# Contiguous Fourier products, one tile left out and a newly searched instruction order in a one-core gated attention and Fourier kernel

## The chip, the cores and the metric

The kernel runs on one core of one Trainium2 chip. The metric is the device time of one launch in microseconds (us). "Before" is the tuned kernel that we start from, "after" is the changed one. Executions of this kernel come in a usual, fast state and in a slower one (over 1.5% above the fastest of the same kernel); the comparisons below use fast runs.

The engines are named as in the profile: PE is TensorE, PEld its weight loads, DVE is VectorE, ACT is ScalarE, POOL is GpSimd, SP is SyncE, which issues most of the transfers.

## The reference

The output mixes two branches of the same input x (2048 rows of 640) with one gate per row. Shapes and masks are cut here to what matters.

```
g = sigmoid((x * gate_w).sum(-1))             # one gate per row
# a: 32 heads of 20 columns, 4 segments of 512 rows, with a running memory
q, k, v = x @ wq, x @ wk, x @ wv
phi = lambda t: where(t > 0, t + 1, exp(t))
for s in range(4):
    p     = softmax(qs @ ks.T * scale + causal_mask)
    a_mem = (phi(qs) @ M) / (phi(qs) @ z)      # M and z are zero in segment 0
    o     = sig(beta) * a_mem + (1 - sig(beta)) * (p @ vs)
    M, z  = M + phi(ks).T @ vs,  z + phi(ks).sum()
a = o @ wo
# b: a spectral filter
b = irfft2(rfft2(x) * (w_r + 1j * w_i))
out = g * a + (1 - g) * b
```

The Fourier transforms are done as matmuls with tables of cosines and sines. Along the 640 columns there are products called D (forward) and Db (inverse); the even and odd symmetry of the input lets each half of a D result be summed from fewer rows.

## The kernel before

The kernel's text is not the order in which its instructions run. The text lists operations (a group of matmuls, an eviction, a transfer) with what they read and write. A list scheduler inside the kernel, called the planner below, then plays the program through when the kernel is built: it has a duration for every operation, starts what is ready by priority, chooses an engine where an operation allows two, gives out PSUM banks, and records what it started. The recorded order is the program. It is fixed: on the chip each engine runs its own list strictly in that order, and waits on semaphores.

```
class Sched:
    HOP = 70.0                        # ns from the end of an operation to its reader
    ...
    def schedule(self, pools, plan=(), nsem=56):
        for o in ops if plan else ():
            shift, pick = divmod(plan[o.key], 3)
            o.prio += shift / 10.0                         # a shift of the priority, us
            if pick and len(o.alts) > 1:                   # and perhaps a pinned engine
                o.alts = dict([list(o.alts.items())[pick - 1]])
        ...
        def try_dispatch(e):
            for idx, o in enumerate(ready[e]):             # sorted by (prio, id)
                if len(o.alts) > 1 and finish(o, e) > min(finish(o, q) for q in o.alts) + 1e-6:
                    continue                               # the other engine ends sooner
                ...
                fn, occ, lat = o.alts[e]
                if e == "pe":
                    occ *= self.pe_slow(now, occ)          # its model of the half clock
                busy_until[e] = now + occ
                ...
                self.order.append(o)
        ...
        self.makespan = max(o.t1 for o in ops)
```

PLAN is a literal of 1324 integers, one for each group of operations, the result of a long search outside the kernel. `makespan` is how long the program takes in the planner's own arithmetic. I shall call it the planned length.

The costs that the planner uses are written beside each operation, for example these two:

```
    def copy_alts(self, dst, src, n, ...):                 # PSUM evictions: either engine
        alts["act"] = (..., 100 + 0.833 * n, 95.0)         # ns occupied, ns of latency
        alts["dve"] = (..., 75 + 1.04 * n, 85.0)
    ...
    # phi: exp on ACT, then max(x, 0) + 1 and a min with the exponential on DVE
    self.Sc.op({"dve": (fmax, 75 + 0.26 * L, 85.0)}, ..., name="phi_max", lock=True)
```

The attention scores run as groups of 4 to 8 small matmuls on row-tiled quarters of the array; the gate tables, the first projections of q and k and the last output projection use column tiles; everything else uses the full array. The 80 score groups share PSUM banks 0 to 3 (one group holds all four), nearly everything else shares banks 4 to 7.

The D products, with their eviction (typ 0 is the cosine part, typ 1 the sine part; KD is 321):

```
    parts = ((0, 0, 2, 161, 0), (1, 0, 1, KD, 161), (2, 1, 2, 160, 482)) if typ == 0 else (
        (2, 1, 2, 160, 642), (3, 0, 1, KD, 802), (4, 0, 2, 161, 1123))
    for n_, (c, c0, st, n, tc) in enumerate(parts):        # chunk, first column, step, columns, table
        th = (self.ps(bank, c0, [st, n]), self.Ac.ap(...), big.ap(tc, [1, n]), n_ == 0, n_ == 2, ...)
        self.mms([(th, n)], ..., name="D")
    copy_alts(Bt.ap(typ * 322, [1, KD]), self.ps(bank, 0, [1, KD]))
```

The first and the third matmul of a group write every second PSUM column (step 2). And the first of the five q tiles of segment 0 is projected, evicted and stored, but nobody reads it.

Of the kernel before, what the change touches and what calls it, by code (L numbers as in the profile page):

```python
# [46 lines left out]
class Op:  # L47
    __slots__ = ("id", "alts", "preds", "succs", "prio", "banks", "nbytes", "npred", "eng", "t0", "t1",
                 "stamp", "need_inc", "dyn", "first", "outside", "name", "dma", "key", "xfer", "lock")


class Sched:
    HOP = 70.0
    WINDOW = 1600000
# [7 lines left out]
    def op(self, alts, r=(), w=(), prio=0.0, nbytes=0, name="", after=(), dma=False, xfer=0.0, lock=False):  # L62
# [6 lines left out]
        o.xfer, o.lock = xfer, lock  # L69
# [39 lines left out]
    def schedule(self, pools, plan=(), nsem=56):  # L109
# [50 lines left out]
        bw_free = port = 0.0  # L160
        sems = [[0.0, i, None] for i in range(nsem)]
# [37 lines left out]
        def try_dispatch(e):  # L199
            nonlocal bw_free, port  # L200
# [6 lines left out]
            for idx, o in enumerate(ready[e]):  # L207
# [31 lines left out]
                if e == "pe":  # L239
                    occ *= self.pe_slow(now, occ)  # L240
# [5 lines left out]
                if o.dma:  # L246
                    bw_free = max(bw_free + o.xfer, now + min(occ, 500.0) + o.xfer, now + occ)
                    tot, i = 0, len(issued) - 1
                    while i >= 0 and tot <= self.WINDOW:
                        tot += issued[i].nbytes  # L250
                        i -= 1
                    if i >= 0:
                        o.dyn.append(issued[i])
                    issued.append(o)
                    flight.append(o)
                    o.t1 = bw_free + 2000.0 + lat
                    sems.sort(key=lambda q: (q[0], q[1]))
                    sm = sems[0]
                    if sm[2] is not None:
                        o.dyn.append(sm[2])  # L260
                    sm[0], sm[2] = o.t1, o
                    o.stamp = sm[1]
                else:
                    o.t1 = busy_until[e] + lat
# [136 lines left out]
def make_tables():  # L401
# [27 lines left out]
    dtab = np.concatenate([C[0:128, 0::2], C[128:256], C[256:384, 1::2], Sn[256:384, 1::2], Sn[384:512], Sn[512:640, 0::2]], 1)  # L429
# [111 lines left out]
PECOL = 0.43  # L541
# [4 lines left out]
class Kern:  # L546
# [35 lines left out]
    def mms(self, items, r, w, prio, name="", extra=0.0):  # L582

        cost = sum(max(c * PECOL, 27.0) for _, c in items) + extra

# [6 lines left out]
        return self.Sc.op({"pe": (f, cost, 110.0)}, r=r, w=w, prio=prio, name=name)  # L592

    def copy_alts(self, dst, src, n, engines=("act", "dve"), scale=None):

        alts = {}
        if "act" in engines:
            alts["act"] = (lambda e: e.activation(dst(), src(), ACT.Copy), 100 + 0.833 * n, 95.0)  # L598
        if "dve" in engines:
            alts["dve"] = (lambda e: e.tensor_copy(dst(), src()), 75 + 1.04 * n, 85.0)  # L600
        return alts

    def one(self, eng, fn, n, r, w, prio, per=None, fix=None, name="", after=()):
        fix0, per0 = {"act": (100, 0.833), "dve": (75, 1.04), "pool": (100, 0.945)}[eng]
        per = per0 if per is None else per
        fix = fix0 if fix is None else fix
        return self.Sc.op({eng: (fn, fix + per * n, 90.0)}, r=r, w=w, prio=prio, name=name, after=after)

    def either(self, fn, n, r, w, prio, name="", after=()):

        return self.Sc.op({"dve": (fn, 75 + 0.52 * n, 90.0), "pool": (fn, 100 + 1.95 * n, 90.0)}, r=r, w=w, prio=prio, name=name, after=after, lock=True)

    def dma(self, dst, src, nbytes, r, w, prio, tr=False, name="", after=(), queue="sp", late=0.0):
        def f(e):
# [3 lines left out]
            with self.nc.allow_non_contiguous_dma(reason="small strided loads"):  # L618
                return e.dma_start(d_, s_)  # L619
        cost = 700.0 + nbytes / 260.0 if tr else 580.0 if nbytes in (41088, 163840) else 430.0  # L620
# [3 lines left out]
                          dma=True, xfer=xfer)  # L624
# [18 lines left out]
        -1614, -1515, -1314, -2268, -2070, -1866, -1878, -1863, -1857, -1815, -1893, -1920, -1356, -750, -231, 99, -3537, -3756, -4283, -4662, -3993,  # L643
        -5778, -5471, -6145, -1554, -2150, -1677, -1437, 189, -2325, -1686, -1374, -2244, -1446, -2277, 39, -3126, -2823, -1632, -3303, -2745, -2856,
        -2076, -1920, -501, -2677, -2334, -2523, -1608, -3204, -1269, -1425, -2984, -1443, -2109, -2759, -3747, -1299, -771, -598, -1323, -2676,
        -2895, -2262, -2847, -1956, -3894, -2832, -3426, -2853, -1347, -432, -757, -864, -3894, -2496, -2355, 1644, 333, 320, -1197, -3672, -2433,
        -3588, -1713, -453, -1851, -3522, -1638, -3057, -1476, -2532, -2439, -1170, -2562, -1761, -2136, -2295, -2844, -1737, -1143, -2541, -387,
        -1668, 1809, -1848, -4359, -2253, -1407, -4161, -3780, -2067, -3582, -3348, -2592, -3678, -2613, -2064, -3219, -3375, -1419, -1947, -1860,
        -3108, -969, -2403, -2538, -2370, -1395, -2427, -2349, -1611, -4107, -3411, -1839, -2328, -2346, -2016, -2661, -2484, -1812, -2409, -2679,
        -1545, -1095, -2184, -2613, -1272, -1026, -3231, -3852, -717, -1917, -2634, -1416, -2151, -1932, -945, -1695, -1923, -816, -555, -2313, -831,  # L650
        -747, -1362, -1002, -1896, -1917, -2424, 105, 498, -2214, -2139, -525, -1440, -2493, -834, 336, -1845, -1923, -132, -1623, -1434, -825, -2466,
        -726, -327, -1311, -1143, -36, -2823, -1578, -516, -384, -3225, -834, 867, -987, -1821, -1257, -264, -2328, 42, -597, -3270, 621, -2175, -312,
        -1737, -79, -2091, 755, -2205, 909, -1866, 1083, -1089, 1011, -1821, 154, -2196, 1341, -1509, 2667, -909, 1379, -1803, 561, -2115, 839, -1371,
        1639, -1797, 2286, -1668, 2085, -1248, 96, -1152, 1375, -951, 863, -723, 1014, -693, 774, -1749, -1581, -750, -652, -1674, -1273, -753, 552,
        -1443, -639, -1130, -483, -1278, -810, -912, -372, -985, -27, 462, -1389, -21, -249, -99, -1114, 99, -856, -2325, -291, 24, -996, 105, -237,
        15, -216, -1184, 63, -686, -378, -911, -573, -1305, 54, 352, -363, -709, -270, -618, -861, -87, 869, -33, -288, -543, 699, -45, -48, -1308,
        633, -537, -18, -1074, -1074, -1381, -819, -231, -9, -966, -123, 1685, 30, -547, -252, -1524, -1503, -468, 1334, -219, 2523, -306, -1125, -90,
        810, -681, 128, -6, -339, 641, 162, 1316, 444, -510, 915, -1242, 285, -998, 366, -70, 312, -180, 585, 693, -108, 705, 1178, 1632, -1566, 363,
        -217, 588, -1412, -285, 1017, 459, 741, 213, 123, 411, 159, -2004, 483, -443, 216, -743, -762, 1821, 1194, 519, 1328, 192, -312, 444, 789,
        447, 1688, 573, 1257, 549, 1302, 730, -129, -424, 105, 1172, -285, 522, 579, 986, 456, 246, 90, 1035, 2255, 603, 872, -54, 788, -474, -1011,  # L660
        513, 2820, 558, 2556, 561, 378, 1143, 516, -1116, -111, -346, 426, -651, 588, 1425, 417, 1262, 300, 1341, 365, 834, -1150, 594, 155, 135,
        -996, 627, 96, 519, 2577, 975, 1380, 1992, 543, -271, 540, 311, 1053, -780, 1488, 1845, 918, 2478, 1722, 4158, 1966, 1035, 13, 1059, -323,
        1218, 546, 1599, 1563, 1371, 1074, 2631, 2838, 2232, 141, 2865, 2742, 2043, 474, 2919, 2775, 2526, 1257, 2544, 2571, 2784, 1239, 2490, 2205,
        3093, -25, 2853, 3045, 2868, 994, 2913, 3528, 3162, 3666, 4401, 3666, 2418, 2494, 5604, 4851, 5259, 3280, 5343, 3417, 5160, 4524, 5151, 4542,
        4197, 2017, 3270, 2574, 3834, 3262, 5250, 3000, 5496, 4156, 5646, 3399, 5187, 2965, 5622, 4614, -1530, -2001, -1172, 1059, -1245, 464, -1515,
        -842, -582, 366, -255, -718, -1881, -1277, -114, -264, -528, -1249, 1023, -2538, -1245, -135, 69, 660, -315, -1596, 666, -4431, 168, 390, 14,
        666, -651, -361, -2280, -1413, 369, 315, 453, 726, -384, -267, -162, 1803, 771, 57, -132, 1332, 216, 783, 2004, 1725, -81, -1413, 1056, 546,
        1048, -1335, -33, -393, -1917, 756, 645, -198, -57, 420, -870, -2073, -783, -792, -1362, -858, -1257, -927, 540, -1257, -780, -1203, -738,
        1011, -1212, -393, -1032, -207, -24, -540, 1155, -2247, -627, -36, -522, 1914, 2535, 18, -843, 2211, 567, 54, -924, 1791, 1950, -315, 699,
        1317, 678, 93, -387, 1941, 1458, 327, 285, 1665, 1236, 456, 2208, 57, 1530, 402, 1422, 57, 1653, -780, 207, -1356, -669, -366, -447, -792,  # L670
        -966, -510, -795, 240, -852, -666, 255, -1662, -849, 468, -2331, 195, -1907, -429, -267, -2631, -753, -969, -345, 39, -69, -303, 696, -858,
        -414, 1302, -1446, -414, 75, 180, -219, -339, -39, -168, 852, -2361, -540, -2190, 345, -243, -1083, -726, -1015, 393, 999, 852, -249, 489,
        -873, 30, -357, 483, -819, -1065, -147, -225, -2067, -1659, 498, 501, -285, 27, 508, -318, 1215, -441, -2235, -563, 714, -579, -945, 312,
# [803 lines left out]
```

## Time and profile before

| before | value |
|---|---|
| time, median of 3 runs before the prediction | 256.04 us (255.57 to 256.52) |
| profiled span, mean granted clock | 255.2 us, 0.993 |
| matmuls | 3248 |
| planned length | 245.2 us |

These are lines of the page of the kernel before. The second gives each engine's busy time, its share of the span and its instructions. The rows are the busy share in tenths in 40 slices of the span, then the granted clock in tenths. The last gives the engines' shares of the chain of work that ended last.

```profile
span 255.2 us, 7980 instructions
...
PE 241.7 (95%) x3248; PEld 142.3 (56%) x3248; DVE 203.2 (80%) x556; ACT 202.8 (79%) x208; POOL 114.2 (45%) x175
...
PE   7999989997999999989989999999998999999994
...
ACT  2397599877899998999988889889889798788710
...
PEclk9999997999999999999999999999999999999999
...
PE 78%; DVE 7%; DMA 5%; ACT 3%; SPq 2%; issue 1%; POOL 1%; ACTq 0%; DVEq 0%
```

TensorE is busy from end to end, the clock is full but for one slice, and the chain runs through TensorE for 78% of the span. ScalarE and VectorE have about 20% to spare, on average.

Groups of instructions of before: line, engine, operation, tiles and shapes, count, then busy us and the mean ns of one, then idle time just before them.

```profile
L590 PE MATMUL psum<-big,Ac 128*128 128x321 bf16 x32 | 10.9, 340 | 0.0
L590 PE MATMUL psum<-big,Ac 128*128 128x161 bf16 x32 | 9.7, 302 | 0.0
...
L600 DVE CAST Bt<-psum 128x321 bf16<-128x321 f32 x17 | 8.3, 488 | 2.1 <-PE psum L590 1.7
L598 ACT ACTIVATE Bt<-psum 128x321 bf16<-128x321 f32 x15 | 6.6, 442 | 1.7 <-PE psum L590 1.4
...
L1062 DVE TENSOR_SCALAR phq<-qu 128x512 bf16<-128x512 bf16 x15 | 5.5, 380 | 0.0
```

Matmuls overlap, so the mean length of one (302 ns for 161 columns) is no measure of the time that it holds the array. Starts are: in the timeline of before a D group starts at 62.84 us and the next matmul at 63.21.

```profile
62.84 0.57 PE L590 MATMUL psum<-big,Ac 128*128 128x161 bf16 x3
...
63.21 0.42 PE L590 MATMUL psum<-wv,xT 128*128 128x500 bf16 x1
```

So three matmuls with 642 columns held the array for about 370 ns. A contiguous 321-column matmul of Db takes 140 ns from start to start in the same trace, so the group should take about 280.

What TensorE waits for in before (us in all, times, longest):

```profile
PE psum L590 <- DVE va L1086: 1.6, 1, 1.6
PE psum L590 <- DVE qu L600: 1.6, 3, 0.8
...
PE psum L590 <- ACT ex L1180: 0.4, 2, 0.2
```

TensorE hardly waits.

### The profile page before, as it was taken

To read this page: it belongs to the slowest core of one execution; us is meant where nothing else is said; L and a number is where in the kernel's file an instruction comes from. 1 tells how busy PE (TensorE), PEld (TensorE's weight loads), DVE (VectorE), ACT (ScalarE), POOL (GpSimd) and SP (SyncE) were. 2 spreads that over 40 slices of the span, in tenths; PEclk is the share of its full clock that TensorE was granted. 3 is DMA by queue.
4 is the path that set the end of the run, shared out by engine and by line. 5 is a ranking of instruction groups with operands and counts; after the bars stand their busy time and mean duration, and the time that the engine had idled before them with its cause. 6 is when DMAs were issued, how large, how long until landed. Compare 5 with 4: busy or idle time off the path is not lost.

```text
span 255.2 us, 7980 instructions
## 1 busy us (share of the span) xinstructions
PE 241.7 (95%) x3248; PEld 142.3 (56%) x3248; DVE 203.2 (80%) x556; ACT 202.8 (79%) x208; POOL 114.2 (45%) x175
## 2 busy tenths in 40 slices
PE   7999989997999999989989999999998999999994
PEld 2344556554666657644655566545564656456583
DVE  0799897768888999899999988989999984625543
ACT  2397599877899998999988889889889798788710
POOL 8015634433532346745255748434665432416400
PEclk9999997999999999999999999999999999999999
DMA  7996979499449356746247484213565303553223
GB/s 181 362 356 189 214 165 238 104 216 225 125 79 243 98 142 187 164 143 172 58 103 177 110 207 104 89 44 113 123 167 167 66 3 81 91 115 96 74 72 103
DMA packets 56003, 36.76 MB, mean 144 GB/s; under 512 B 31792, under 2 KB 52256, under 8 KB 55968
## 3 DMA queue, kind: packets, MB, share of 16 engines
q1 hardware_dynamic: 54272, 35.45, 55.1%
q10 hardware_dynamic: 1696, 0.82, 1.2%
q8 instruction: 25, 0.41, 0.7%
q14 instruction: 10, 0.08, 0.1%
HBM read 19.86 MB, written 9.84 MB: 116 GB/s over the span
## 4 chain that ended last, share of the span: by engine, by line
PE 78%; DVE 7%; DMA 5%; ACT 3%; SPq 2%; issue 1%; POOL 1%; ACTq 0%; DVEq 0%
PE psum L590 78%; DMA pkn<-phk 3%; ACT ex L1180 2%; SPq L619 2%; DVE Pt L1329 2%; DMA tt<-tab_tt 1%; DMA kp<-k_scr 1%; DVE va L1086 1%; DVE mem L1123 1%; POOL Yt L1334 1%; DVE Cp L600 1%; DVE G L1375 1%; ACT eo L598 1%; DVE qu L600 1%; POOL ex L1183 1%
## 5 line engine op out<-in xcount | busy, mean ns | idle before, releaser
L1180 ACT ACTIVATE ex<-psum 128x2048 bf16<-128x2048 f32 x80 | 150.3, 1879 | 19.2 <-PE psum L590 18.7
L1183 POOL TENSOR_SCALAR_AFFINE_SELECT ex<-ex 128x512 bf16<-128x512 bf16 x128 | 80.7, 648 | 111.3 <-ACT ex L1180 108.8
L590 PEld LDWEIGHTS psum<-va,ex 128*128 128x128 bf16 x1280 | 36.7, 96 | 6.7 <-issue 1.5
L590 PE MATMUL psum<-va,ex 128*128 128x21 bf16 x1280 | 38.6, 172 | 1.0 <-POOL ex L1183 0.3
L590 PE MATMUL psum<-qp,kp 20*128 20x512 bf16 (+3 forms) x512 | 31.9, 303 | 1.4 <-DMA kp<-k_scr 0.8
L590 PE MATMUL psum<-xT,wk 128*128 128x512 bf16 (+1 forms) x140 | 28.6, 381 | 1.3 <-DVE qu L600 0.8
L590 PE MATMUL psum<-xT,wq 128*128 128x512 bf16 (+1 forms) x140 | 28.3, 381 | 0.2 <-DVE Pt L1329 0.2
L590 PE MATMUL psum<-wv,xT 128*128 128x141 bf16 (+1 forms) x160 | 28.0, 306 | 0.0
L1329 DVE TENSOR_TENSOR Pt<-psum,Wt 128x642 bf16<-128x642 f32 x32 | 25.6, 821 | 2.1 <-PE psum L590 1.9
L590 PE MATMUL psum<-wo,oT 128*128 128x320 bf16 x120 | 22.1, 301 | 0.0
L590 PEld LDWEIGHTS psum<-qp,kp 20*128 20x128 bf16 x512 | 8.9, 92 | 21.4 <-ACT ex L1180 9.3
L590 PE MATMUL psum<-big,Ac 128*128 128x161 bf16 (+2 forms) x96 | 18.6, 316 | 0.7 <-DVE qu L600 0.6
L590 PEld LDWEIGHTS psum<-wv,xT 128*128 128x128 bf16 x160 | 13.2, 99 | 9.2 <-issue 1.2
L590 PE MATMUL psum<-big,Cp 128*128 128x321 bf16 (+1 forms) x96 | 17.2, 302 | 1.0 <-DVE eo L600 0.4
L1051 ACT ACTIVATE et<-qu 128x512 bf16<-128x512 bf16 x25 | 15.6, 630 | 2.7 <-DVE qu L600 2.5
L1086 DVE TENSOR_TENSOR va<-psum,ebx 128x500 bf16<-128x500 f32 (+1 forms) x32 | 15.2, 481 | 3.2 <-PE psum L590 2.3
L600 DVE CAST ot<-psum 128x320 bf16<-128x320 f32 x19 | 9.1, 490 | 10.6 <-PE psum L590 9.5
L590 PEld LDWEIGHTS psum<-xT,wk 128*128 128x128 bf16 (+1 forms) x140 | 9.8, 98 | 12.9 <-issue 2.2
L1375 DVE TENSOR_TENSOR G<-eo,psum 128x320 bf16<-128x320 f32 x32 | 14.6, 475 | 2.5 <-PE psum L590 2.4
L590 PEld LDWEIGHTS psum<-xT,wq 128*128 128x128 bf16 (+1 forms) x140 | 10.3, 98 | 11.2 <-issue 1.6
L1215 DVE TENSOR_TENSOR on<-psum,rs 128x320 bf16<-128x320 f32 x32 | 15.4, 482 | 0.3
L590 PE MATMUL psum<-tt,Yt 128*128 128x256 bf16 (+1 forms) x96 | 15.3, 276 | 0.1
(80 smaller groups left out, 360.0 us busy)
## 6 DMA issues: line engine op xcount, KB each, us to landing
tt<-tab_tt SPq DMA_DIRECT2D x16, 256.0 KB, 3.0
xsb<-in_A_x_dram SPq DMA_DIRECT2D x8, 320.0 KB, 6.8
qp<-q_scr SPq DMA_DIRECT2D x28, 80.0 KB
kp<-k_scr SPq DMA_DIRECT2D x28, 80.0 KB
o_scr<-on SPq DMA_DIRECT2D x12, 160.0 KB
out_dram<-ot SPq DMA_DIRECT2D x12, 160.0 KB
q_scr<-qu SPq DMA_DIRECT2D x6, 256.0 KB
k_scr<-qu SPq DMA_DIRECT2D x6, 256.0 KB, 2.8
```

What stands on the lines that cost most here:

```text
L590: h = e.matmul(o_, l_, r_, start=st, stop=sp_, **kw)
L598: alts["act"] = (lambda e: e.activation(dst(), src(), ACT.Copy), 100 + 0.833 * n, 95.0)
L600: alts["dve"] = (lambda e: e.tensor_copy(dst(), src()), 75 + 1.04 * n, 85.0)
L619: return e.dma_start(d_, s_)
L1051: self.one("act", lambda e: e.activation(et.ap(0, [1, L]), qsl(), ACT.Exp), L, [qb], [b("et", pi_)], late, name="phi_exp")
L1086: self.one("dve", lambda e: e.tensor_tensor(va.ap(i * H * VW + h0 * VW, [VW, nh], [1, DH]), self.ps(bank, 0, [DH, nh], [1, DH]), self.ebx. ...
L1123: self.one("dve", lambda e: e.tensor_tensor(self.mem.ap(i * D + q * 320, [DH, 16], [1, DH]), self.ps(bank, 0, [VW, 16], [1, DH]), dn.ap(16 ...
L1180: self.one("act", lambda e: e.activation(dst(), src(), ACT.Exp, scale=SC), 4 * width, [bank], [self.exb(s, g, j) for g, j in outs], prio - ...
L1183: self.one("pool", lambda e, g=g, j=j: e.affine_select(self.ex.ap(self.exo(s, g) + JOFF[j], [1280, 4], [1, P]), self.ex.ap(self.exo(s, g) ...
L1215: self.one("dve", lambda e, rs=rs, bank=bank, g=g: e.tensor_tensor(on.ap(80 * g, [D, 4], [DH, 4], [1, DH]), self.ps(bank, 0, [88, 4], [VW, ...
L1329: self.one("dve", lambda e, ri=ri, Pt=Pt, Wt=Wt, bank=bank: e.tensor_tensor(Pt.ap(ri * 322, [644, 2], [1, KD]), self.ps(bank, 0, [0, 2], [ ...
L1375: self.one("dve", lambda e, q=q, n2=n2, bank=bank, eo=eo: e.tensor_tensor(self.G.ap(n2 * D + 639 * q, [1 - 2 * q, 320]), eo.ap(q, [1, 320] ...
```

## The change

It has four parts. (1) Each D group writes contiguous PSUM columns, odd results first and even ones after, and the eviction puts them back in order. (2) The unread q tile is dropped. (3) The planner's model gets a charge of 95 ns for each change of array tiling, a new column cost, new latencies and transfer issue times, and the right to put the max of phi on GpSimd. (The model of before has no such charge; it adds a fixed 120 ns to each score group and 80 ns to each group of gate products instead.) (4) PLAN is replaced by one said to be searched anew. The core of the diff, with cuts:

```
 class Sched:
     HOP = 70.0
+    SWITCH = 95.0
...
                 if e == "pe":
+                    if o.mode != pe_mode:
+                        occ += self.SWITCH
+                        pe_mode = o.mode
                     occ *= self.pe_slow(now, occ)
...
-    dtab = np.concatenate([C[0:128, 0::2], C[128:256], C[256:384, 1::2], Sn[256:384, 1::2], ...], 1)
+    oe = np.concatenate([od, ev])
+    dtab = np.concatenate([C[0:128, 0::2], gap, C[128:256][:, oe], gap, C[256:384, 1::2], ...], 1)
...
-PECOL = 0.43
+PECOL = 1.0 / 2.4
...
-            alts["act"] = (..., 100 + 0.833 * n, 95.0)
+            alts["act"] = (..., 65 + 0.833 * n, 110.0)
-            alts["dve"] = (..., 75 + 1.04 * n, 85.0)
+            alts["dve"] = (..., 67 + 1.04 * n, 68.0)
...
     def proj_tile(self, s, which, t, prio, xT, xb):
+        if s == 0 and which == "q" and t == 0:
+            return
...
-            self.Sc.op({"dve": (fmax, 75 + 0.26 * L, 85.0)}, ..., name="phi_max", lock=True)
+            self.Sc.op({"dve": (fmax, 67 + 0.26 * L, 68.0), "pool": (fmax, 100 + 0.98 * L, 50.0)}, ..., name="phi_max", lock=True)
...
-                parts = ((0, 0, 2, 161, 0), (1, 0, 1, KD, 161), (2, 1, 2, 160, 482)) ...
+                parts = ((0, 160, 161, 0), (1, 0, KD, 162), (2, 0, 160, 484)) ...
-                        return (self.ps(bank, c0, [st, n]), ...
+                        return (self.ps(bank, c0, [1, n]), ...
-                copy_alts(Bt.ap(typ * 322, [1, KD]), self.ps(bank, 0, [1, KD]), KD)
+                copy_alts(Bt.ap(typ * 322 + 1, [-1, 2], [2, 161]), self.ps(bank, 0, [160, 2], [1, 161]), 322)
...
     PLAN = (
-        -1614, -1515, -1314, -2268, ...          # 1324 numbers, from -6145 to 12456
+        ...                                      # 1322 numbers, from -27442 to 24697
```

## The prediction

> **What bounds the kernel now.** TensorE. The page gives it 241.7 of 255.2 us busy (95%), VectorE and ScalarE 203 each, GpSimd 114; the chain of waits is 78% TensorE. Busy time of pipelined matmuls overstates, so I added up start-to-start intervals of the trace's 3248 matmuls (249.7 us, first start to last): about 206 us are columns at full rate; about 21 us are extra intervals at 208 changes between full-array, row-tiled (attention scores) and column-tiled matmuls, 95 to 100 ns each (a 512-column matmul is followed after 216 ns, before a change after 311 to 317); 3 us belong to the Fourier D groups; 15 us are other gaps, of which 2.5 us the slow warm-up and 1.7 us a half-clock window near 41 to 44 us. The waits view shows little else: 1.7 us on a V eviction, under 1 us each on a load of k, q evictions, W products.
>
> **What the change does.**
> 1. D products. Each of 32 groups is a 161-, a 321- and a 160-column matmul; the short ones write every second PSUM column. Their intervals are 96, 178 and 96 ns, 370 together. A contiguous 321-column matmul (the inverse D products) takes 140, a contiguous 154-column one 67; so contiguous halves should take 70+140+70, about 279 ns. 32 x 91 ns = 2.9 us. The Trainium skill, "PSUM — Partial Sum Buffer", Specifications, says that any non-contiguous access pattern slows matmuls significantly; this trace agrees, by 26 ns on 161 columns. The interleaving moves to the eviction (485 ns on VectorE, 442 on ScalarE); I expect it no longer, and neither engine is the limit.
> 2. Dropped q tile: 5 x 216 ns = 1.1 us of TensorE in the first 26 us, where it runs almost without a break; also one 0.6 us eviction and 128 KB of store.
> 3. New order. The search now charges 95 ns per tiling change, and has other DMA issue times and latencies. The Trainium skill, "TensorEngine Tiling (Array Packing)", Key Properties, says changing the tiling mode drains the engine; the 100 ns agree. The 80 score units share one set of four PSUM banks, so most of their 160 changes stay. The 24 column-tiled gate products before the output projection cost two changes each; pairing them with each other or with score units could save 10 to 25 changes, 1 to 2.5 us. Of about 10 us of real gaps I expect 2 to 4 to go.
>
> **Critical path.** Items 1 and 2 lie on it fully, since TensorE is saturated when they run: 4.0 us. Item 3 is worth 3 to 7, and could be zero or negative where real landings differ from the model's. Start and tail (4 us after the last matmul starts) stay.
>
> **Prediction: 247.0 us** (256.0 - 4.0 - 5.0), range 242 to 252 for 8 in 10. Faster by over 2%: 0.78; within 2%: 0.20; slower: 0.02.
>
> **What would show it.** 3243 matmuls; D intervals near 70/140/70; D evictions still at 485/442 ns; fewer than 200 tiling changes; TensorE gaps from 15 to near 11 us; chain still above 75% TensorE.
>
> **What would make it wrong.** The halves do not speed up because the slowness came from elsewhere; the strided bf16 write lengthens evictions; the new order waits on a DMA or eviction the model takes as early, or lets TensorE idle into another half-clock window (1.7 us each); or the search found much more (below 242) by grouping tiling changes.

## The result, and the profile after

| | before | after |
|---|---|---|
| median | 256.28 us (255.57 to 257.26, 4 runs) | 310.16 us (308.26 to 316.74, 4 runs, one of them slow) |
| ratio of fast runs, 95% interval | | 1.208 (1.2029 to 1.2131) |
| profiled span, mean granted clock | 255.2 us, 0.993 | 308.6 us, 0.91 |
| matmuls | 3248 | 3243 |
| planned length | 245.2 us | 286.6 us |

A ratio in this document is the mean time of one kernel's fast runs over the mean of the other's fast runs of the same rounds, so it is not quite the ratio of the medians beside it. All kernels except one marked as wrong gave the right result.

The change makes the kernel 54 us slower where I had predicted 9 us faster. The lines of the page after that answer to those of before:

```profile
span 308.6 us, 7952 instructions
...
PE 253.0 (82%) x3223; PEld 144.5 (47%) x3243; DVE 201.0 (65%) x520; ACT 207.7 (67%) x217; POOL 152.2 (49%) x201
...
PE   8798779988977994987898969899899849973486
...
ACT  1668476876988663588779938875887726935721
...
PEclk9999999997999799799999979955999968996559
...
PE 39%; DVE 16%; ACT 14%; DMA 12%; POOL 11%; SPq 4%; issue 3%; DVEq 0%; ACTq 0%; POOLq 0%
```

No engine is near its limit any more. VectorE's work is the same as before, 201 us, and ScalarE's nearly so; there is no new heavy work but 38 us on GpSimd. The chain has left TensorE (78% to 39%) and wanders over all engines: everybody waits for somebody. (The 20 matmuls that are missing from the first count are lost records; the weight loads count 3243.)

The groups after:

```profile
L600 PE MATMUL psum<-big,Ac 128*128 128x321 bf16 x32 | 9.8, 307 | 0.0
...
L610 DVE CAST Bt<-psum 128x322 bf16<-128x322 f32 x17 | 8.6, 512 | 1.2 <-PE psum L600 1.1
L608 ACT ACTIVATE Bt<-psum 128x322 bf16<-128x322 f32 x15 | 8.0, 542 | 0.8 <-PE psum L600 0.8
L600 PE MATMUL psum<-big,Ac 128*128 128x161 bf16 x32 | 7.6, 239 | 2.6 <-DVE Pt L1349 1.8 <-ACT Bt L608 0.3 <-DVE on L1234 0.2
...
L1083 POOL TENSOR_SCALAR phq<-qu 128x512 bf16<-128x512 bf16 x7 | 13.6, 1943 | 3.6 <-DVE qu L610 1.6 <-PE psum L600 1.2 <-ACT qu L608 0.7
L1083 POOL TENSOR_SCALAR phk<-qu 128x512 bf16<-128x512 bf16 x5 | 9.9, 1971 | 2.4 <-ACT qu L608 1.4 <-DMA pkn<-phk 0.7 <-DVE qu L610 0.3
```

Three things are to be read here. The D matmuls did get shorter: 302 to 239 ns in the mean of the 161-column ones, and from start to start, as medians by width (161, 321 and 160 columns), 80, 141 and 79 ns where before had 96, 178 and 96 (in the first experiment 70, 141 and 71 in the undisturbed groups). The evictions got longer: 442 to 542 ns on ScalarE, 488 to 512 on VectorE. And 15 of the 30 max operations of phi (three more are in a third group) went to GpSimd, where one takes 1.94 us instead of the 0.28 to 0.38 us on VectorE; the planner counts 100 + 0.98 * 512 ns, which is 0.60 us.

TensorE's waits after:

```profile
PE psum L600 <- ACT ex L1199: 14.2, 12, 5.1
PE psum L600 <- DMA oT<-o_scr: 5.6, 3, 4.1
PE psum L600 <- DVE Pt L1349: 4.3, 7, 1.2
PE psum L600 <- DMA tt<-tab_tt: 4.1, 2, 2.9
```

The wait on the exponentials rose from 0.4 to 14.2 us, although ScalarE has more free time than before. The longest one shows how that can be, in the timeline after, whose columns are start, duration, engine and instruction, and in brackets the idle time before it and what ended it.

```profile
276.12 0.85 PE L600 MATMUL psum<-wo,oT 128*128 128x320 bf16 x5
278.12 0.44 ACT L608 ACTIVATE ot<-psum 128x320 bf16<-128x320 f32 x1 [4.99 <-DMA out_dram<-ot]
...
279.78 0.44 ACT L608 ACTIVATE ot<-psum 128x320 bf16<-128x320 f32 x1 [1.23 <-DMA out_dram<-ot]
...
280.12 1.87 ACT L1199 ACTIVATE ex<-psum 128x2048 bf16<-128x2048 f32 x1
282.04 0.14 PEld L600 LDWEIGHTS psum<-qp,kp 20*128 20x128 bf16 x8 [5.40 <-ACT ex L1199]
282.04 0.61 PE L600 MATMUL psum<-qp,kp 20*128 20x384 bf16 x8 [5.07 <-ACT ex L1199]
```

ScalarE's list has two output evictions ahead of the exponential. Each needs a buffer that a store to memory still holds, so ScalarE stands for 4.99 us and then for 1.23; the exponential behind them, which needs no such thing, comes late; the four score banks stay full; TensorE's next instruction is a score group, and TensorE stands for 5.07 us. None of these operations is slow in itself. The order is wrong for what really happens.

Stretches of 30 us as a table: window, length, then busy us (and instructions) of PE, PEld, DVE, ACT and POOL, then the mean clock, the transfer share and GB/s. First before, then after.

```profile
core 0: us, PE busy (x) PEld busy (x) DVE busy (x) ACT busy (x) POOL busy (x), PEclk, DMA share, GB/s
...
180.00:210.00 30.00, 28.12 (x385) 16.29 (x382) 27.20 (x84) 25.84 (x25) 16.67 (x23) 1.00 0.44 111
210.00:240.00 30.00, 30.00 (x436) 16.76 (x433) 14.83 (x35) 23.52 (x21) 12.52 (x19) 1.00 0.42 94
```

```profile
180.00:210.00 30.00, 26.91 (x293) 14.39 (x296) 19.36 (x45) 21.66 (x22) 16.67 (x22) 0.81 0.43 79
...
270.00:300.00 30.00, 17.32 (x307) 10.59 (x308) 7.47 (x19) 15.04 (x14) 9.62 (x15) 0.67 0.20 44
```

The second cost is the clock. After has the clock at 0.81 and 0.67 of full in these stretches, where before has 1.00 in its own. By the records, the half clock is granted for 55.5 us of after, in stretches of one, two, four or six times 3.41 us (the last one is cut off by the end), against 3.4 us of before.

For the whole run I added up the start-to-start intervals of all matmuls, and split each into columns at full rate (n columns at 2.4 per ns and 2.7 ns), the extra of the half clock, the extra at a change of tiling, the extra of the D groups, and the rest, which are gaps:

| us | before | after |
|---|---|---|
| columns at full rate | 204.7 | 199.5 |
| extra of the half clock | 4.1 | 14.1 |
| changes of tiling | 20.6 (208 of them) | 19.1 (184) |
| extra of the D groups | 3.1 | 1.2 |
| gaps | 17.3 | 70.1 |
| first to last matmul | 249.7 | 303.9 |

(The split is mine; where a wait and a half clock or a change of tiling meet, it is a choice by 1 or 2 us.) About 4 us of after's gaps are the 20 lost records. The rest is clear: what the change set out to save, it saved (1.9 us in the D groups, about 1 us of columns, 24 tiling changes or 1.5 us), and 49 us of waiting and 10 us of half clock came on top.

### The profile page after: what moved, and what is told of

It is laid out like the page before. It is cut to its first block, busy times and chain, and to the rows that moved or that the text cites. A ratio compares the mean times of both kernels' runs of the same rounds, so it can differ in the third digit from the quotient of the medians.

```text
span 308.6 us, 7952 instructions
## 1 busy us (share of the span) xinstructions
PE 253.0 (82%) x3223; PEld 144.5 (47%) x3243; DVE 201.0 (65%) x520; ACT 207.7 (67%) x217; POOL 152.2 (49%) x201
## 4 chain that ended last, share of the span: by engine, by line
PE 39%; DVE 16%; ACT 14%; DMA 12%; POOL 11%; SPq 4%; issue 3%; DVEq 0%; ACTq 0%; POOLq 0%
PE psum L600 39%; ACT ex L1199 11%; POOL phq L1083 3%; SPq L629 3%; DVE Pt L1349 3%; DMA tt<-tab_tt 3%; DMA xsb<-in_A_x_dram 2%; DMA oT<-o_scr 2%; DMA out_dram<-ot 2%; POOL ex L1202 2%; POOL phk L1083 2%; DMA gbc<-g_scr 1%; DVE phk L1084 1%; POOL xsb L927 1%; POOL xf L922 1%
## 5 line engine op out<-in xcount | busy, mean ns | idle before, releaser
L600 PE MATMUL psum<-qp,kp 20*128 20x384 bf16 (+3 forms) x512 | 34.3, 324 | 14.5 <-ACT ex L1199 14.2
L600 PE MATMUL psum<-wv,xT 128*128 128x500 bf16 (+1 forms) x160 | 29.9, 312 | 4.2 <-DVE Ac L610 2.8
L600 PE MATMUL psum<-xT,wk 128*128 128x512 bf16 (+1 forms) x127 | 26.2, 387 | 4.3 <-DMA wk<-in_A_wk_dram 1.9
L600 PE MATMUL psum<-xT,wq 128*128 128x512 bf16 (+1 forms) x128 | 25.3, 384 | 2.1 <-DVE q L610 0.5
L600 PE MATMUL psum<-big,Cp 128*128 128x321 bf16 (+1 forms) x96 | 21.2, 355 | 0.2
L1229 DVE TENSOR_TENSOR rs<-psum,gate 128x16 f32<-128x16 f32 x32 | 5.4, 169 | 24.2 <-PE psum L600 23.9
L600 PE MATMUL psum<-tt,Yt 128*128 128x256 bf16 (+1 forms) x96 | 16.9, 296 | 2.3 <-DVE qu L610 0.7
L600 PE MATMUL psum<-big,Ac 128*128 128x161 bf16 (+2 forms) x96 | 15.3, 262 | 3.0 <-DVE Pt L1349 1.8
L600 PE MATMUL psum<-Bt,tt 128*128 128x321 bf16 x64 | 13.2, 306 | 5.2 <-DMA tt<-tab_tt 4.1
L600 PEld LDWEIGHTS psum<-wo,oT 128*128 128x128 bf16 x120 | 11.2, 102 | 13.2 <-DMA oT<-o_scr 6.5
```

What stands on the lines that cost most here:

```text
L600: h = e.matmul(o_, l_, r_, start=st, stop=sp_, **kw)
L1229: self.one("dve", lambda e, rs=rs, bank=bank: e.tensor_tensor(rs.ap(16, [4, 4], [1, 4]), self.ps(bank, DH, [88, 4], [VW, 4]), self.g1.ap(4 ...
```

## The experiments

Two theories stood at first. Theory A: the data edits are sound, and the delivered order is bad, because the plan does not fit the planner that it is delivered with. Theory B: something in the edits or in the new model costs time whatever the plan (the longer evictions, the max on GpSimd, the new costs). The planned length spoke for A: by the planner's own arithmetic after takes 286.6 us, and only 270.8 with no plan at all.

### The data edits alone, in the order of before

**e1_halves.** The kernel before with part 1 only. The planner's costs are left as they were, so that the order is before's instruction for instruction.

```
-    parts = ((0, 0, 2, 161, 0), (1, 0, 1, KD, 161), (2, 1, 2, 160, 482)) ...
+    parts = ((0, 160, 161, 0), (1, 0, KD, 162), (2, 0, 160, 484)) ...
     # and the reordered table and the interleaving eviction of the change; cost of the eviction unchanged
```

> The kernel before, with the D products in two contiguous halves and nothing else; every engine's order, engine choice and PSUM bank is that of before. Theory A (the new order costs the time, the other two edits are worth what was predicted): 253.1 us, ratio 0.988 to before (32 x 91 ns less on TensorE); D intervals 70/140/70. Rival C (the interleaving eviction, 542 ns instead of 442 on ScalarE in the changed kernel, hurts): 256 us or more.

Measured: 254.28 us against 256.37 of before, ratio 0.9933 (0.9883 to 0.9982). The D intervals are 70, 141 and 71 ns. The evictions, in the groups of this kernel:

```profile
L603 DVE CAST Bt<-psum 128x322 bf16<-128x322 f32 x17 | 8.8, 519 | 0.8 <-PE psum L593 0.8
L601 ACT ACTIVATE Bt<-psum 128x322 bf16<-128x322 f32 x15 | 8.0, 538 | 0.6 <-PE psum L593 0.5
```

So the part works: 88 ns on each of 32 groups are 2.8 us on TensorE, and about 2 of them reach the end (0.5 to 3 by the interval). The longer evictions are real here too.

**e2_halves_drop.** e1 and part 2: the operations of the unread tile are planned as before and then left out of the program, so that the rest keeps its order.

```
+        self.order = [o for o in self.order if not o.skip]     # their waits are handed on
```

> The same, and the unread q tile left out of the emitted program, the order of all else held. Theory A: 252.0 us, ratio 0.984. Rival C: 255 or more.

Measured: 254.34 us, ratio 0.9917 (0.986 to 0.9974). Against e1 nothing that these runs resolve; the 1.1 us of the dropped tile do not show at the end. Both data edits together are worth about 2 us (0.7 to 3.6 by the interval), half of the 4.0 predicted. They are no cause of the loss: theory B loses its first suspect.

### The plan alone

**e3_no_plan.** The kernel after, scheduled without PLAN.

```
-    self.Sc.schedule({"qk": [0, 1, 2, 3], "gen": [4, 5, 6, 7]}, self.PLAN)
+    self.Sc.schedule({"qk": [0, 1, 2, 3], "gen": [4, 5, 6, 7]})
```

> The changed kernel with its plan taken away (all shifts zero, engine choices free), the changed cost model kept. The planner's own makespan falls from 286.6 to 270.8 us. Theory A (the plan delivered does not fit the program it is delivered with): faster than the changed kernel, 285 to 297 us. Rival B (the changed cost model misjudges the chip, so that its better orders are no better on it): 305 us or more.

Measured: 278.61 us, ratio 1.0851 (1.0780 to 1.0923); planned 270.8. Taking the new plan away makes the kernel 31 us faster, more than theory A had expected (285 to 297 us). The delivered plan is worse than none.

**e4_old_plan.** The kernel after with before's PLAN (less the two entries of the dropped tile).

> The changed kernel with the plan of before (its two entries for the dropped tile removed), the changed cost model kept. The planner's own makespan is 259.5 us. Theory A: 268 to 280 us, well below the changed kernel's 310 although that plan was made for another model. Rival B: 300 us or more.

Measured: 274.24 us, ratio 1.0641 (1.0561 to 1.0721); planned 259.5. A plan is tied to the model that it was searched with: the same numbers that give 256 us with the old model give 274 with the new one, and even the delivered numbers are worse than these.

### The max of phi on GpSimd

**e5_phi_dve.** The order of after is kept, but the 15 max operations that it puts on GpSimd are emitted on VectorE.

```
+    for o in self.Sc.order:
+        if o.name == "phi_max" and o.eng == "pool":
+            o.alts, o.eng = {"dve": o.alts["pool"]}, "dve"
```

> The changed kernel, its order of issue held, but the 15 phi maximum operations that it sends to GpSimd (1.94 us each in its trace, while its planner charges 0.60) are emitted on VectorE (0.35 us each). Rival B (the misjudged phi maximum is what makes the new order slow): below 285 us. Theory A (the order is bad already by its own planner, 286.6 us against 245.2; the misjudged operation is only an extra): 293 to 305 us, some 5 to 16 us less than the changed kernel's 310.

Measured: 304.14 us, ratio 1.1801 (1.1704 to 1.1898). In the groups of this kernel all 15 of one kind are on VectorE:

```profile
L1087 DVE TENSOR_SCALAR phq<-qu 128x512 bf16<-128x512 bf16 x15 | 5.7, 383 | 0.7 <-ACT qu L608 0.7
```

The gain is 6 us of the 54. The wrong cost is an error, and a measurable one, but a small part of the loss. Theory B's second suspect explains a ninth.

### How firmly the plan holds

**e6_hop60.** The kernel after with one constant of the planner changed by 10 ns, the hop from an operation's end to its reader.

```
-    HOP = 70.0
+    HOP = 60.0
```

> The changed kernel with one constant of the planner changed, HOP from 70 to 60 ns; plan and all else as delivered. The planner's own makespan falls from 286.6 to 269.4 us, only because the order comes out otherwise. Theory A (the delivered plan is no optimum of the delivered planner; almost any disturbance gives a better order, and the planner's makespan foretells the direction on the chip): 278 to 298 us. Rival B (planner and chip have parted company): no relation, 305 to 315.

Measured: 295.38 us, ratio 1.149 (1.1403 to 1.1577); planned 269.4 instead of 286.6. Ten nanoseconds in one constant of the model reshuffle the order, and move the chip's time by 14 us. The delivered plan is not an optimum of its planner, since a random small change helps; and any plan is fragile, since before's own planned length goes from 245.2 to 255.6 if its hop is made 71 (a number of the build; not run).

### Do the longer evictions cost?

**e7_halves_plain_evict.** e1 with a straight eviction. The columns stay in the wrong order, so the result is wrong (relative error 1.41).

```
-    copy_alts(Bt.ap(typ * 322 + 1, [-1, 2], [2, 161]), self.ps(bank, 0, [160, 2], [1, 161]))
+    copy_alts(Bt.ap(typ * 322, [1, KD]), self.ps(bank, 0, [1, KD]))
```

> Wrong result on purpose. The halves alone in the order of before (as the first run), but the eviction of the D products copies the 321 columns straight instead of interleaving them. It prices the interleaving eviction. If its extra 96 ns on ScalarE and 31 ns on VectorE are what kept the halves at 254.3 us (0.993) where 253.1 was expected: 253.3 us, ratio 0.988 to 0.990, evictions at 442 and 488 ns. If the eviction is off the critical path: 254.3, ratio 0.993, as the first run.

Measured: 254.19 us, ratio 0.9914 (0.9854 to 0.9975). The evictions are back at 439 ns (ScalarE) and 486 ns (VectorE), so the interleaving is what lengthens them:

```profile
L603 DVE CAST Bt<-psum 128x321 bf16<-128x321 f32 x17 | 8.3, 486 | 1.0 <-PE psum L593 1.0
L601 ACT ACTIVATE Bt<-psum 128x321 bf16<-128x321 f32 x15 | 6.6, 439 | 0.8 <-PE psum L593 0.6
```

In time it can't be told from e1: inconclusive, and by the two intervals hardly above 2 us.

### A plan that fits its planner

**e8_new_plan.** The kernel after with nothing changed but the numbers of PLAN: I searched for a plan on the delivered planner. Planned 247.1 us, 195 changes of tiling.

> The changed kernel with only the numbers of its plan replaced, by a plan that I searched for this very program with this very planner (annealing from the plan of before). The planner's makespan is 247.1 us instead of 286.6, with 195 tiling changes. Theory A (the delivered plan does not fit; the other edits and the cost model are sound): 253 to 260 us, ratio 0.99 to 1.015, more than 50 us under the changed kernel. Rival B (the changed cost model leads astray on the chip): 270 us or more.

Measured: 272.75 us (268.53 to 275.31), ratio 1.0532 (1.0417 to 1.0648). Four of the six runs were slow, so the ratio rests on two, with a mean of 270.2 us. Against the fast runs of after (309.5) a fitting plan wins back 39 us. But that is not what theory A had expected (253 to 260); it is at the line of rival B (270 or more), and it misses its planned length by 23 us, where before misses its own by only 11. TensorE's waits in this kernel:

```profile
PE psum L600 <- DVE va L1119: 2.4, 4, 1.0
PE psum L600 <- DVE Pt L1361: 2.1, 7, 0.6
PE psum L600 <- DVE mem L1156: 2.0, 4, 0.9
```

The waits are spread, and VectorE is at the head of them. So theory A is half of the answer. The other half may be that the new model itself is too cheap somewhere; the next runs test that.

**e9_new_plan_no_switch.** The same search, with the charge for a change of tiling set to zero in both search and schedule. Planned 244.6 us, 212 changes.

```
-    SWITCH = 95.0
+    SWITCH = 0.0
```

> The same search, with as many trials, but the planner charges nothing for a tiling change (SWITCH 0); its makespan is 244.6 us, in which 212 changes are free. If the charge is worth having in the model: 258 to 268 us, slower than the run with the charge by 3 us or more, with 10 to 20 more tiling changes in the trace. If it isn't: within 2 us of that run.

Measured: 281.0 us, ratio 1.0905 (1.0803 to 1.1007), about 10 us above e8 by the fast runs (279.8 against 270.2). The charge did no harm and seems to help. Seventeen changes fewer at 95 ns are only 1.6 us; the rest may be that times in the model are then nearer to the chip's, or the luck of one search each. One pair doesn't separate these.

### Orders searched on corrected costs

I compared the planner's durations with the traces and raised them: every VectorE operation by 12 ns, those which the planner locks against GpSimd by 35 to 100 ns more, GpSimd's folds by 450 ns (a fold of 640 columns takes 1.96 us in the trace of after, where the planner counts 1.32). I kept the max of phi on VectorE, and let the search shift each operation by itself and not by group. The kernel then carries the order itself:

```
-    self.Sc.schedule({"qk": [0, 1, 2, 3], "gen": [4, 5, 6, 7]}, self.PLAN)
+    self.Sc.replay(self.ORDER, self.BANKS)       # explicit order, engines and banks
```

**e10_robust_order** was searched under random delays as well; **e11_tight_order** without. Planned 246.4 and 241.1 us.

> The changed kernel's program (halves, dropped tile), issued in an explicit order per operation, searched on a cost model corrected by the traces (every VectorE operation 12 ns more; phi maximum kept off GpSimd; [...]GpSimd folds 450 ns more; the interleaving eviction at its measured length), scored as the mean over six replays of the order with random delays. By that score it is about 9 us under the order of before (256.8 to 266.0). Theory D (orders searched on the delivered planner fail on the chip because its costs are too low and nothing in the score stands for jitter): 244 to 251 us, ratio 0.955 to 0.98. If the planner of the change is not to blame for the 25 us that the new plan lost on the chip: 262 us or more.

> The same with the same corrected costs, but searched for the bare makespan without random delays (241.1 us by the corrected model against 246.4 for the run above and 254.9 for the order of before). It tells the two halves of theory D apart. If the corrected costs are what matters: 242 to 250 us, within 3 us of the run above. If the tightness of an order searched without delays is what failed: 255 us or more.

Measured: 257.07 us, ratio 0.9973 (0.9910 to 1.0035), and 257.36 us, ratio 0.9936 (0.9862 to 1.0010). By the ratios both are 14 to 15 us below e8 and level with before. Both miss what I had expected (244 to 251 us, and 242 to 250): the corrected orders win back the loss, but not the gain. Half the runs of e11 were slow. The random delays in the search made no difference that these runs resolve. The first waits of TensorE in e10:

```profile
PE psum L633 <- DMA tt<-tab_tt: 3.7, 2, 2.1
PE psum L633 <- DVE Pt L1440: 1.6, 2, 1.2
```

VectorE's waits have shrunk, and the load of a Fourier table leads, where before waits 0.2 us on it. The gaps are 26.7 us in e10 and 25.7 in e11 (whose profiled run was a slow one), against 17.3 of before; about 4 and 5 us of them are lost records, 19 and 23 matmuls.

**e12_landings** and **e13_landings_tight.** The same two searches, with every transfer landing 0.8 us later in the model and 3 ns more for each matmul group. Planned 248.4 and 248.3 us.

> As the robust order, but in the searched model every DMA lands 0.8 us later and every group of matmuls costs 3 ns more, and four replays with random delays make up the score; by it the order is 12 us under that of before (257.9 to 270.2), and without delays 7 us (248.4 to 255.1). If late landings are what cost the two orders before it their gain (their traces wait 4 to 6 us on the T tables, the order of before 0.2): 248 to 252 us, ratio 0.965 to 0.985. If not: 255 to 258 again.

> The same model with late landings, searched from the order of before for the bare makespan (248.3 us; the order of before 255.1). If the later landings matter and random delays do not: 248 to 252 us, as the run above. If the score with delays matters: 3 us or more slower than the run above.

Measured: 256.03 us, ratio 0.9951 (0.9891 to 1.0012), and 255.00 us, ratio 0.9915 (0.9857 to 0.9973). (One run of before took 732.95 us; it counts as slow and is left out.) In e12 TensorE still waits longest on the load that I had meant to cover; in e13 on another:

```profile
PE psum L633 <- DMA tt<-tab_tt: 6.8, 3, 2.7
```

```profile
PE psum L633 <- DMA oT<-o_scr: 2.2, 1, 2.2
```

Expected were 248 to 252 us for both. So later landings in the model are not what was missing, or not by that amount. e13 is level with e2: the best versions are 0.8% below before, which is real by the intervals but within 2%. No version beats before clearly.

## Why the prediction was wrong, and where it was right

The kernels in one table. The chip's time is the mean of the fast runs. The difference in the last column but one is that mean less the planned length: how far each order falls short of what its planner believed. In brackets stand the gaps less the 19 or 20 lost records of a trace, about 4 us. (The profiled runs of e4, e8 and e13 fell 1.5 to 2.5 us above their medians; their gaps are counted from those. The calls ran on different chips, so small differences between rows are better read from the ratios.)

| kernel | planned | chip | difference | gaps in the trace |
|---|---|---|---|---|
| before | 245.2 | 256.3 | 11 | 17.3 |
| after | 286.6 | 309.5 | 23 | 70.1 (66) |
| e3, no plan | 270.8 | 278.2 | 7 | 33.6 (29) |
| e4, before's plan | 259.5 | 273.3 | 14 | 40.6 (36) |
| e6, hop 60 | 269.4 | 295.7 | 26 | 52.7 |
| e8, plan searched on this planner | 247.1 | 270.2 | 23 | 33.6 |
| e9, the same without the charge | 244.6 | 279.8 | 35 | 39.0 |
| e10, corrected costs | 246.4 | 256.3 | 10 | 26.7 (23) |
| e13, corrected costs, later landings | 248.3 | 254.5 | 6 | 20.0 |

**The step that failed** is the third: "New order", with the sentences "Item 3 is worth 3 to 7, and could be zero or negative where real landings differ from the model's" and "Of about 10 us of real gaps I expect 2 to 4 to go". The measured worth of the new order is the difference between after and e2, which holds the same data edits in the old order: by the ratios 1.208 and 0.9917, a loss of about 55 us. The gaps did not fall by 2 to 4 us; they rose from 17 to about 66, without the lost records. A new order that waits on evictions and transfers stood among the risks, but at 0.02 for any result slower by over 2%. The sentence rests on a premise that I did not state and did not test: that a plan delivered as "searched anew" is a good plan for the planner beside it.

**What the runs showed in its place.** Most of the 54 us are the numbers of the plan. By one and the same model the delivered plan takes 286.6 us and one searched for it 247.1, which is 39 us less before any question of what the chip does; on the chip the fast runs of these two kernels differ by 39 us as well (309.5 against 270.2). Taking the plan away altogether won 31 us. What remains is a second loss: with a fitting plan the chip still took 23 us more than planned, and orders searched on corrected costs and operation by operation took 14 to 15 us less. These two things were changed together, so I can't share the 15 us between them, and that the model's costs are to blame is likely but not shown. The misjudged max of phi is 6 us of after's loss by e5. What is left after that, beside e2, is at most 1.4 us by the ratios.

**Why so little disorder costs so much** is in the profile after: the engines run fixed lists, so a late transfer at the head of ScalarE's list (4.99 us) held an exponential behind it, and through the full score banks TensorE (5.07 us). The clock fell with the waits. I had named such a window as a risk at 1.7 us each; there were 55.5 us of half clock in all, and 14.1 us of extra column time. The Trainium skill, "TensorE: Matmul & The Clock Gate", Part 1, gives half clock as the default and after at least one idle window of about 3.4 us. The stretches of 3.41 us agree. But no window had to be wholly idle. Cut into windows of 3.41 us, with n columns counted as n/2.4 ns and twice that at half clock, the traces of before and after show the clock falling after windows in which columns streamed for up to 0.38 of the time (0.44 in one window of e6); in after it came back after windows with 0.76 and more, but also stayed down through windows with up to 0.84. So gaps of a sixth to a quarter of the time could hold it down.

**Point by point.**
- D groups: predicted 370 to 279 ns, measured 282 in e1. Right. The Trainium skill, "PSUM — Partial Sum Buffer", Specifications, says that a non-contiguous access pattern slows matmuls significantly; here it took 96 instead of 70 ns at 161 columns, and 178 instead of 141 for the 321-column matmul between the two.
- Worth of both data edits: predicted 4.0 us, measured about 2 (e1 and e2). The mechanism holds, the size is half: "Items 1 and 2 lie on it fully" was too much. In e1 TensorE's wait on the exponentials grows from 0.4 to 1.2 us and that on q evictions from 1.6 to 2.3: part of the gain turned into waits at the same places. In e7, with the short evictions, the wait on the exponentials is back at 0.4 us, but that on q evictions is 2.9; these are single profiled executions, and the missing 2 us stay unexplained.
- "I expect it no longer" of the eviction: wrong. It grew by 100 ns on ScalarE and 24 to 31 on VectorE (e1), and e7 shows that the interleaving does it. Its cost in time is not resolved.
- Fewer than 200 tiling changes: right (184), and worth 1.5 us as costed. The Trainium skill, "TensorEngine Tiling (Array Packing)", Key Properties, says that a change of mode drains the array; the 95 to 104 ns of extra for each change agree (20.6 us for 208, 19.1 for 184).
- 3243 matmuls: right.
- "TensorE gaps from 15 to near 11 us; chain still above 75% TensorE": wrong, about 66 us and 39%.

**What stays open.** On what the delivered plan was searched isn't to be found from these runs. A hint was in the diff: in before 134 of the 1324 numbers are not divisible by 3, which is what pins an engine; in after 881 of 1322, two thirds, as random numbers would have, and the range is nearly three times as wide. That suits a plan made for other keys or for another decoding, but it is an argument, not a finding. Open too is why even orders on corrected costs lose 7 to 16 us to their model, and why before, whose model is cruder, loses no more.

## What to carry to other kernels

Where a kernel's order is made from a table of search results, the table and the model are one thing: check, each time either is changed, the planner's own length, and compare the new table with no table in the same model (here 286.6 against 270.8), before anyone asks what the chip does. In a static order, a cost that the model puts too low can hold up the lists of other engines; so measure each operation that the model newly allows on an engine before a search may use it (here 15 operations at 1.94 us against 0.60, which cost 6 us at the end). And judge data edits in the old order: two sound edits worth 2 us were hidden under a loss of 55.

## What the Trainium skill lacked or had wrong

- "GPSIMD Engine Reference", 4.1 Engine selection, calls elementwise operations with one input on GpSimd roughly line-rate. Here a one-input max and add over 128x512 bf16 took 1.94 us on GpSimd and 0.28 to 0.38 us on VectorE.
- "TensorE: Matmul & The Clock Gate", Part 1, gives a window of idle time as what halves the clock, and tells of a kernel whose frequent short idle times did it, but has no figure for how much idle time suffices. Here the clock halved after windows of 3.41 us in which columns streamed for up to 0.38 of the time (0.44 once), and came back somewhere between 0.76 and 0.84.
- "PSUM — Partial Sum Buffer", Specifications, has no figure for the slowdown. Here writing every second fp32 column took 96 instead of 70 ns at 161 columns, and slowed the contiguous matmul between two such ones as well (178 against 141 ns).
- "TensorEngine Tiling (Array Packing)", Key Properties, has no figure for the drain. Here a change of tiling cost 95 to 104 ns.
- No page gives the cost of an interleaving eviction. Here 128x322 from PSUM to every second bf16 column took 538 to 542 ns on ScalarE and 512 to 519 on VectorE, against 442 and 488 for 128x321 written straight.
